# Two feed-forward blocks behind attention: the magnitude step of the second weight block queued behind the exponentials on ScalarE

## The chip, the cores and the metric

The kernel runs on one core of a Trainium2 chip. Five engines work side by side, each through its own instructions in order: TensorE (PE, matrix products), VectorE (DVE), ScalarE (ACT), GpSimd (POOL) and SyncE (SP, which issues the loads here). The metric is the device time of one execution in microseconds (us); the time given is the median of three runs.

## What is computed

Attention over 8 heads and 2 batches (576 positions, 64 dimensions), a sum of a coarse attention over positions averaged by four and of a local one within three positions; then a feed-forward layer of width 2048 with a squared rectifier; then a mixture of four experts of width 1024.

```python
x = attn_ref(q, k, v)                     # 1152 x 512, coarse + local attention
r = np.maximum(x @ w_in, 0.0)
g = s * (r * r) + b
x = g @ w_out
p = domain_probs / domain_probs.sum(-1, keepdims=True)
for e in range(4):
    h = np.maximum(x @ w1[e], 0.0)
    out += p[:, e:e + 1] * (h @ w2[e])
```

The weights of the first layer, `w_in` and `w_out`, come as 64-bit floats, which the kernel takes as pairs of 32-bit words.

## The kernel before

**The stages.** Attention comes first, in 16 units: a unit is two heads of one half of a batch, and four units make a group of columns. The feed-forward layer runs in four blocks of 512 hidden columns, and each block has two layers: layer 1 makes four chunks of hidden values, and layer 2 multiplies them with the second weights. Block 0 is done group by group while attention still runs: as soon as the four units of a group are done, its layer 1 and layer 2 products (L316) are strewn between the next units' steps. Blocks 1 to 3 and the mixture of experts follow.

**A unit's steps** are spread over the passes of one loop (`for i in range(last + 1)`): scores of one unit are written ahead (`b_step`, with the exponentials `exps` at L571 on ScalarE), then the transposes of the probabilities (`c_step`, L657 and L660), the products with the values (`d_step`, L678, L685, L694, L701), and the rounding into the layer's input (`x_step`: L713 on ScalarE, then L715 on POOL). For every other group POOL also makes the averaged keys and values (L474, L475, L539, L541). VectorE takes maxima (L615, L617) and normalises (L630 to L635).

**A hidden chunk** (`moe1_l1`) goes from TensorE through L767 (rectifier, ScalarE), L769 (square and scale, VectorE), L772 (the high part of `h`, ScalarE) and L773 (its low part, VectorE). Each layer 2 product takes three terms of every chunk, in the order high, low, high (`PAIRS`). L793 copies the layer 2 sum away.

**A weight quarter** is converted by `prep`: the magnitude of the high word (`magnitude`, L157, ScalarE), a clamp (L161), a shift (L167) and two joinings with the raw words (L175 and L186, all on VectorE), the high part (L196, ScalarE) and the low part (L199, VectorE), behind which the next raw quarter is loaded into the freed buffer (L122, SP). The steps are taken one at a time from a list (`side_step`) after an attention step or a piece of a block. A block has four quarters, named (block, layer, half). Those of block 1's layer 1, (1, 0, 0) and (1, 0, 1), enter the list at pass i = 12, those of its layer 2 after the loop.

**What sets the order.** The kernel is written in this order, but a scheduler that knows dependences and an estimate of the durations sorts the instructions on each engine; so a step that is written late can be queued early where its inputs are there. `tc.issue_after(x)` holds an instruction back in that sorting until `x` has been placed. On POOL the order is that of the code (`manual_schedule`).

Of the kernel before, what the change touches and what calls it, by code (L numbers as in the profile page):

```python
# [8 lines left out]
F32 = mybir.dt.float32  # L9
# [3 lines left out]
ACTF = mybir.ActivationFunctionType  # L13
# [9 lines left out]
def attn_moe_moe_kernel(  # L23
# [14 lines left out]
    nc = tc.nc  # L38
# [36 lines left out]
    def window(n):  # L75

        return min(max(n * TQ - FAC, 0), S - W)

    def f32(ap):
        return ap.bitcast(F32)  # L80
# [19 lines left out]
    def load_next():  # L100
        if not stream:
            return
        n, which, half = stream.pop(0)
        wi, wo, f0 = blocks[n]
        m = 2 if n < n_moe1 else 1
        dt = I32 if n < n_moe1 else F32
        if n < n_moe1:
            wi, wo = wi.bitcast(I32), wo.bitcast(I32)
        f0 += half * 256
        if which == 0:  # L110
            src = wi[:, f0 * m : (f0 + 256) * m].rearrange("(k p) f -> p k f", p=P)
        else:
            src = wo[f0 : f0 + 256, :].rearrange("(c p) d -> p c d", p=P)
        if n < n_moe1:
            t = rawp.tile([P, 2048], dt, tag="raw", name="raw")
        else:
            if "raw2" not in pools:
                t = rawp.tile([P, 2048], dt, tag="raw", name="raw2")
                pools["raw2"] = [t[:, :1024], t[:, 1024:]]
            t = pools["raw2"].pop(0)  # L120
            pools["raw2"].append(t)
        nc.sync.dma_start(out=t.rearrange("p (a b) -> p a b", a=src.shape[1]), in_=src)  # L122
        raw[n, which, half] = t
# [4 lines left out]
    def w_slot(which):  # L128
        i = places[which].pop(0)
        places[which].append(i)  # L130
        if i < 3 - which:
            pool = wp1 if which else wp0
        else:
            pool = pools["wy" if which else "wx"]
        return [
            pool.tile([P, 1024], F32R, tag=f"w{which}{c}{i}", name=f"w{which}{c}", bufs=1)
            for c in range(2)
        ]

    def prep(n, which, half):  # L140

        if n >= n_moe1:
            return prep2(n, which, half)
        parts = w_slot(which)
        wt[n, which, half] = parts
        st = {}

        def words():
            w = raw[n, which, half].rearrange("p (n two) -> p n two", two=2)
            return w[:, :, 0], w[:, :, 1]  # L150

        def magnitude():
            f = rawp.tile([P, 1024], F32, tag="cv", name="cv")
            st["f"] = f
            nc.scalar.activation(out=f, in_=words()[1].bitcast(F32), func=ACTF.Abs)  # L157

        def clamp():
            f = st["f"]  # L160
            nc.vector.tensor_scalar(  # L161
                out=f, in0=f, scalar1=2.0**-15, scalar2=122879.9921875, op0=ALU.max, op1=ALU.min
            )

        def join():
            c = st["f"].bitcast(I32)
            nc.vector.tensor_scalar(  # L167
                out=c,
                in0=c,
                scalar1=5,  # L170
                scalar2=2,
                op0=ALU.logical_shift_left,
                op1=ALU.logical_shift_right,
            )
            nc.vector.scalar_tensor_tensor(  # L175
                out=c,
                in0=words()[0],
                scalar=29,
                in1=c,
                op0=ALU.logical_shift_right,  # L180
                op1=ALU.bitwise_or,
            )

        def sign():
            c = st["f"].bitcast(I32)
            nc.vector.scalar_tensor_tensor(  # L186
                out=c,
                in0=words()[1],
                scalar=-(2**30),
                in1=c,  # L190
                op0=ALU.bitwise_and,
                op1=ALU.bitwise_or,
            )

        def high():
            nc.scalar.copy(parts[0], st["f"])  # L196

        def low():
            nc.vector.tensor_tensor(  # L199
                out=parts[1], in0=st["f"], in1=f32(parts[0]), op=ALU.subtract  # L200
            )
            load_next()
            ready.add((n, which, half))


        nonlocal tail
        steps = [magnitude] + tail[:1] + [clamp] + tail[1:] + [join, sign]
        tail = [high, low]
        return steps
# [138 lines left out]
    nc.vector.memset(idle, 0.0)  # L348

    last_pe = {}  # L350
    firsts = []

    def take_slot():
# [44 lines left out]
    def unit(u):  # L398
        g, j = divmod(u, NP)
        b, hf = divmod(g, HALVES)  # L400
        return g, j, b, hf

    def tiles(hf):

        return (0, CUT) if hf == 0 else (CUT, NTQ - CUT)
# [6 lines left out]
    def bank():  # L412
        return psa.tile([P, 512], F32, tag="a", name="psa")
# [137 lines left out]
    def b_step(u):  # L551

        g, j, b, hf = unit(u)
        n0, m = tiles(hf)
        gd = m * TQ // FAC
        qz, qd = st.pop(("q", u))
        kT = st["kT", j]
        kd = st["kd", j]
        pl = ap2.tile([P, MX, W], F32, tag="pl", name="pl")[:, :m]
        ml = ap2.tile([P, MX, 1], F32, tag="ml", name="ml")[:, :m]  # L560
        both = gd == GB
        pd = ap2.tile([P, 2, SD], F32, tag="pd", name="pd")
        md = ap2.tile([P, 2, 1], F32, tag="md", name="md")
        if both:
            pd, md = pd[:, :1], md[:, :1]
        else:
            pd, md = pd[:gd], md[:gd]
        sm = sums[u % 2]

        def exps(out, ps, m, total):  # L570
            nc.scalar.activation(  # L571
                out=out, in_=ps, func=ACTF.Exp, bias=m, scale=1.0, accum_out=total
            )

        ps = [bank()] + ([] if both else [bank()])
        last_pe["att"] = nc.tensor.matmul(
            ps[0][:, : m * W],
            identb.rearrange("p a q -> p (a q)"),
            mask[:, hf * 2 : hf * 2 + m].rearrange("p t w -> p (t w)"),
            start=True,  # L580
            stop=False,
        )
        for _ in range(fill[u] // 448):
            nc.tensor.matmul(
                ps[0][:, : m * W], idle[:, :P], idle[:, : m * W], start=False, stop=False
            )
        for t in range(m):
            k0 = window(n0 + t)
            for a in range(2):
                o = slice(a * D, a * D + D)  # L590
                last_pe["att"] = nc.tensor.matmul(  # L591
                    ps[0][a * TQ : a * TQ + TQ, t * W : t * W + W],
                    qz[o, t * TQ : t * TQ + TQ],
                    kT[o, k0 : k0 + W],
                    start=False,
                    stop=t == m - 1,
                )
        local = ps[0][:, : m * W].rearrange("p (t w) -> p t w", w=W)
        pooled = [] if both else [ps[0][:gd, MX * W : MX * W + SD], ps[1][:gd, :SD]]
        if both:  # L600
            pooled = [ps[0][: 2 * gd, MX * W : MX * W + SD]]
            for a in range(2):
                o = slice(a * D, a * D + D)
                last_pe["att"] = nc.tensor.matmul(
                    ps[0][a * gd : a * gd + gd, MX * W : MX * W + SD],
                    qd[o, :],
                    kd[o, :],
                    start=True,
                    stop=True,
                )  # L610
        else:
            for a in range(2):
                o = slice(a * D, a * D + D)
                last_pe["att"] = nc.tensor.matmul(pooled[a], qd[o, :], kd[o, :], start=True, stop=True)
        nc.vector.tensor_reduce(out=ml, in_=local, axis=AX.X, op=ALU.max, negate=True)  # L615
        for a in range(len(pooled)):
            nc.vector.tensor_reduce(  # L617
                out=md[:, a], in_=pooled[a], axis=AX.X, op=ALU.max, negate=True
            )
        for t in range(m):  # L620
            exps(pl[:, t], local[:, t], ml[:, t], sm[:, t])
        for a in range(len(pooled)):
            exps(pd[:, a], pooled[a], md[:, a], sm[: pd.shape[0], MX + a])
        st["p", u] = pl, pd
# [509 lines left out]
```

## Time and profile before

| | us |
|---|---|
| median of three runs (685.72 to 687.32) | 686.23 |
| the profiled execution | 685.9 |
| its span | 684.1 |
| TensorE busy in the span | 673.0 (98%) |
| VectorE busy | 404.7 (59%) |
| ScalarE busy | 345.2 (50%) |
| POOL busy | 103.0 (15%) |

The span is what the records of the engines cover; the profiled execution's own time is 1.8 us longer. Attention with block 0 lasts to about 135 us, block 1 follows. Busy shares are means over the span: in the first 100 us VectorE and ScalarE are busy for 75% and 69%, behind it for about half.

### The profile page before, as it was taken

The numbers are of one execution on the slowest core, as the hardware profiler recorded it, in microseconds if no ns is written. First come the engines' busy times: TensorE is split into PE (matmuls) and PEld (weight loads), VectorE is DVE, ScalarE is ACT, GpSimd is POOL, SyncE is SP. The second block draws the span as 40 slices with busy tenths as digits, with TensorE's granted clock in tenths as the row PEclk, the third lists the DMA queues.
The fourth block names the chain that finished last, engine by engine and source line by source line (L and its number), as shares of the span: only waits on it lengthen the run. The fifth ranks groups of instructions, "written<-read, shape, count | busy, mean of one in ns | idle before, by whom it ended". The sixth has DMA issues, their size and how long they took to land.

```text
span 684.1 us, 11957 instructions
## 1 busy us (share of the span) xinstructions
PE 673.0 (98%) x4788; PEld 614.5 (90%) x4788; DVE 404.7 (59%) x720; ACT 345.2 (50%) x846; POOL 103.0 (15%) x123
## 2 busy tenths in 40 slices
PE   9879999999999999999999999999999999999997
PEld 6668888999999999999899998898998999988996
DVE  1899878598834425695525645646456365455442
ACT  3777788787956656754443433334234234343220
POOL 4431540100002001021201201210112012010000
PEclk9999999999999999999999999999999999999999
DMA  9975845133500101000301201101102012011012
GB/s 189 229 173 112 145 130 157 63 120 127 184 1 1 32 1 62 1 32 0 86 9 61 63 31 32 62 32 61 32 32 65 29 32 92 27 36 32 1 62 77
DMA packets 54167, 46.43 MB, mean 68 GB/s; under 512 B 32224, under 2 KB 42720, under 8 KB 54112
## 3 DMA queue, kind: packets, MB, share of 16 engines
q1 hardware_dynamic: 54112, 45.67, 24.5%
q8 instruction: 37, 0.61, 0.4%
q14 instruction: 18, 0.15, 0.1%
HBM read 43.31 MB, written 2.36 MB: 67 GB/s over the span
## 4 chain that ended last, share of the span: by engine, by line
PE 89%; DVE 7%; ACT 2%; issue 1%; POOL 1%; POOLq 0%; ACTq 0%
PE psm L316 43%; PE psx L863 26%; PE psx L316 13%; PE psa L361 2%; PE psa L591 1%; PE psa L657 1%; DVE cv L175 1%; PE psa L685 1%; PE psa L512 1%; DVE cv L167 1%; PE psa L494 1%; PE psa L678 1%; DVE cv L186 1%; DVE cv L161 0%; DVE pl L632 0%
## 5 line engine op out<-in xcount | busy, mean ns | idle before, releaser
L316 PE MATMUL psm<-w,h 128*128 128x512 f32 x864 | 208.7, 391 | 0.0
L316 PEld LDWEIGHTS psm<-w,h 128*128 128x128 f32 x864 | 158.5, 188 | 30.0
L863 PE MATMUL psx<-x,w 128*128 128x320 f32 (+1 forms) x768 | 117.7, 296 | 0.0
L863 PEld LDWEIGHTS psx<-x,w 128*128 128x128 f32 x768 | 109.2, 189 | 1.7
L259 POOL TENSOR_TENSOR sw<-raw 128x256 f32<-128x256 f32 x32 | 30.1, 960 | 412.1 <-DMA raw<-in_moe_w_dram 270.3
L878 ACT COPY r<-psx 128x320 f32<-128x320 f32 (+1 forms) x96 | 38.1, 396 | 92.9 <-PE psx L863 92.5
L881 ACT ACTIVATE h<-r 128x320 fp32r<-128x320 f32 (+1 forms) x96 | 42.1, 444 | 82.8 <-DVE r L892 82.8
L934 DVE SCALAR_TENSOR_TENSOR acc<-psm,pr,acc 128x512 f32<-128x512 f32 x63 | 47.2, 749 | 57.1 <-PE psm L316 57.1
L863 PE MATMUL psx<-t,w 128*128 128x320 f32 (+1 forms) x448 | 80.2, 302 | 0.3 <-DVE r L892 0.3
L892 DVE TENSOR_TENSOR r<-psx,r 128x320 f32<-128x320 f32 (+1 forms) x96 | 43.2, 456 | 57.9 <-PE psx L863 56.3
L863 PEld LDWEIGHTS psx<-t,w 128*128 128x128 f32 x448 | 67.0, 188 | 4.6 <-DVE r L892 0.6
L316 PE MATMUL psm<-x,w 128*128 128x320 f32 (+2 forms) x420 | 66.6, 310 | 0.0
L316 PEld LDWEIGHTS psm<-x,w 128*128 128x128 f32 x420 | 62.3, 189 | 0.3 <-issue 0.2
L882 DVE SCALAR_TENSOR_TENSOR h<-r,h 128x320 fp32r<-128x320 f32 (+1 forms) x96 | 48.2, 508 | 18.5 <-ACT h L881 16.4
L316 PE MATMUL psm<-h,w 128*128 128x256 f32 (+2 forms) x360 | 56.1, 305 | 0.3 <-DVE h L773 0.3
L316 PE MATMUL psx<-h,w 128*128 128x384 f32 (+1 forms) x312 | 55.8, 327 | 0.0
L316 PEld LDWEIGHTS psx<-h,w 128*128 128x128 f32 x312 | 52.0, 188 | 0.0
L316 PEld LDWEIGHTS psm<-h,w 128*128 128x128 f32 x360 | 50.9, 190 | 1.0 <-DVE h L773 0.5
L316 PE MATMUL psx<-x,w 128*128 128x384 f32 (+2 forms) x252 | 43.1, 320 | 0.0
L316 PEld LDWEIGHTS psx<-x,w 128*128 128x128 f32 x252 | 40.6, 188 | 0.0
L237 DVE TENSOR_TENSOR w<-raw,w 128x1024 fp32r<-128x1024 f32 x16 | 19.5, 1224 | 26.7 <-ACT w L234 26.7
L780 DVE TENSOR_TENSOR h<-r,h 128x384 fp32r<-128x384 f32 (+2 forms) x40 | 21.6, 541 | 20.9 <-ACT h L779 19.6
(105 smaller groups left out, 865.8 us busy)
## 6 DMA issues: line engine op xcount, KB each, us to landing
raw<-in_moe_w_dram SPq DMA_DIRECT2D x32, 512.0 KB
raw<-in_moe_w_in_dram SPq DMA_DIRECT2D x8, 1024.0 KB
raw<-in_moe_w_out_dram SPq DMA_DIRECT2D x8, 1024.0 KB
kn<-in_k_dram SPq DMA_DIRECT2D x8, 288.0 KB
v<-in_v_dram SPq DMA_DIRECT2D x8, 288.0 KB
out_dram<-acc SPq DMA_DIRECT2D x9, 256.0 KB
qn<-in_q_dram SPq DMA_DIRECT2D x8, 160.0 KB
vn<-in_v_dram SPq DMA_DIRECT2D x16, 72.0 KB
```

The source lines that it names most:

```text
L167: nc.vector.tensor_scalar(out=c, in0=c, scalar1=5, scalar2=2, op0=ALU.logical_shift_left, op1=ALU.logical_shift_right,)
L237: nc.vector.tensor_tensor(out=k0[1], in0=source(), in1=f32(k0[0]), op=ALU.subtract)
L259: nc.gpsimd.tensor_tensor(out=operand(out), in0=operand(x), in1=operand(y), op=op)
L316: nc.tensor.matmul(o, stat(ps, kk), mov(pm, kk, i), start=c == 0, stop=c == len(terms) - 1)
L361: nc.tensor.matmul(ps[:, c0:], idle[:, :P], idle[:, :n], start=True, stop=True)
L780: nc.vector.tensor_tensor(out=h[1], in0=r, in1=f32(h[0]), op=ALU.subtract)
L863: nc.tensor.matmul(ps, s_ap(n, half, a, w, kk), xt[x, pi][b][:, kk], start=first and c == 0, stop=c == len(terms) - 1, skip_group_check=True,)
L878: nc.scalar.copy(t, st[name])
L881: nc.scalar.activation(out=h[0][:, halves[hf]], in_=t, func=ACTF.Relu)
L882: nc.vector.scalar_tensor_tensor(out=h[1][:, halves[hf]], in0=t, scalar=0.0, in1=f32(h[0][:, halves[hf]]), op0=ALU.max, op1=ALU.subtract,)
L892: nc.vector.tensor_tensor(out=st[t], in0=st[name], in1=st[t], op=ALU.add)
L934: nc.vector.scalar_tensor_tensor(out=a, in0=ps, scalar=p_e, in1=a, op0=ALU.mult, op1=ALU.add)
```

## The change

The call that writes the magnitude of a quarter is put under `issue_after` where the block is 1, and every exponentials call notes its instruction, so that the four magnitudes of block 1 are placed behind the last exponentials written ahead of them: those of unit 11 and 12 for layer 1, and of unit 15 for layer 2.

```diff
         def magnitude():
             f = rawp.tile([P, 1024], F32, tag="cv", name="cv")
             st["f"] = f
-            nc.scalar.activation(out=f, in_=words()[1].bitcast(F32), func=ACTF.Abs)
+            with tc.issue_after(last_act["att"].ins) if n == 1 else nullcontext():
+                nc.scalar.activation(out=f, in_=words()[1].bitcast(F32), func=ACTF.Abs)
...
+    last_act = {}
...
         def exps(out, ps, m, total):
-            nc.scalar.activation(
+            last_act["att"] = nc.scalar.activation(
                 out=out, in_=ps, func=ACTF.Exp, bias=m, scale=1.0, accum_out=total
             )
```

The line numbers of the new kernel are one more behind L157 and two more behind L350. The scheduler sorts again, so more rows move than the four that are held.

In the rows below `cv` is a quarter's buffer under conversion, `raw` its raw words, `w` with a number its high and low parts; `r` and `h` belong to a hidden chunk, `pl` and `pd` to the probabilities of a unit.

VectorE before, where the first magnitude of block 1 stood at 61 us of the trace (`cv_1590`; `w11_306` is the last quarter of block 0, `h_897` with `r_975` the low part of a fourth chunk):

```order
L769 SCALAR_TENSOR_TENSOR r_975<-r_975,s_sb_90 128x256
L701 TENSOR_TENSOR xg_1003<-psa_981,ud_1001 128x320
L630 TENSOR_SCALAR sum0_106<-sum0_106 128x7
L161 TENSOR_SCALAR cv_1590<-cv_1590 128x1024
L773 SCALAR_TENSOR_TENSOR h_897<-r_975,b_sb_91,h_896 128x256
L631 RECIPROCAL sum0_106<-sum0_106 128x7
L615 TENSOR_REDUCE ml_1052<-psa_1055 128x5
L199 TENSOR_TENSOR w11_306<-cv_788,w10_305 128x1024
L632 TENSOR_TENSOR pl_918<-pl_918,sum0_106 128x360
```

The same place on VectorE in the changed kernel:

```order
L771 SCALAR_TENSOR_TENSOR r_975<-r_975,s_sb_90 128x256
L703 TENSOR_TENSOR xg_1003<-psa_981,ud_1001 128x320
L632 TENSOR_SCALAR sum0_106<-sum0_106 128x7
L633 RECIPROCAL sum0_106<-sum0_106 128x7
L200 TENSOR_TENSOR w11_306<-cv_788,w10_305 128x1024
L775 SCALAR_TENSOR_TENSOR h_897<-r_975,b_sb_91,h_896 128x256
L634 TENSOR_TENSOR pl_918<-pl_918,sum0_106 128x360
```

The clamp of block 1 is gone from here, and the low part of block 0's last quarter stands ahead of the fourth chunk's low part, no longer behind it.

TensorE before, at the same place (`psm_1019` is the layer 2 sum that takes the fourth chunk; `kn` and `idle` rows are an attention unit's transposes and fillers, of which the middle is left out):

```order
L614 MATMUL psa_1056<-kd3_485,qd_960 80x144
L316 MATMUL psm_1113<-h_858,w10_303 128x256
L494 MATMUL psa_1082<-ident_79,kn_910 128x96 x3
...
L494 MATMUL psa_1090<-ident_79,kn_910 128x96
L316 MATMUL psm_1019<-h_896,w10_305 128x256
L316 MATMUL psm_1019<-h_897,w10_305 128x256
...
L316 MATMUL psm_1019<-h_896,w11_306 128x256
L316 MATMUL psm_1019<-h_896,w10_305 128x256
L316 MATMUL psm_1019<-h_897,w10_305 128x256
L316 MATMUL psm_1019<-h_896,w11_306 128x256
```

TensorE there in the changed kernel:

```order
L616 MATMUL psa_1055<-kd3_485,qd_960 80x144
L317 MATMUL psm_1019<-h_896,w10_305 128x256
L317 MATMUL psm_1019<-h_897,w10_305 128x256
L616 MATMUL psa_1056<-kd3_485,qd_960 80x144
L496 MATMUL psa_1082<-ident_79,kn_910 128x96 x3
...
L317 MATMUL psm_1019<-h_896,w11_306 128x256
L317 MATMUL psm_1019<-h_896,w10_305 128x256
L496 MATMUL psa_1090<-ident_79,kn_910 128x96 x2
L317 MATMUL psm_1019<-h_897,w10_305 128x256
L317 MATMUL psm_1019<-h_896,w11_306 128x256
```

All six products of the third and fourth chunk have moved ahead of the second set of the unit's transposes and fillers.

ScalarE before, from the exponentials of unit 11 to the fourth chunk of the third group (`h_1614`; the third chunk is the one with `r_1616`, the fourth the one with `r_1666`):

```order
L571 ACTIVATE pd_1569,sum1_107<-psa_1571,md_1570 128x144
L767 ACTIVATE r_1616<-psm_1601 128x320
L694 ACTIVATE ud_1638<-psa_1622 128x64
L772 ACTIVATE h_1614<-r_1616,b_sb_91 128x320
L660 COPY pT_1642<-psa_1643 72x512
L660 COPY pT_1642<-psa_1649 72x256
L713 CAST x0_76<-xg_1640 128x256
L767 ACTIVATE r_1666<-psm_1653 128x320
L196 CAST w00_1565<-cv_1718 128x1024
L772 ACTIVATE h_1614<-r_1666,b_sb_91 128x320
```

The same stretch of ScalarE in the changed kernel:

```order
L573 ACTIVATE pd_1569,sum1_107<-psa_1571,md_1570 128x144
L158 ACTIVATE cv_1590<-raw_908 128x1024
L769 ACTIVATE r_1616<-psm_1601 128x320
L696 ACTIVATE ud_1638<-psa_1622 128x64
L662 COPY pT_1642<-psa_1643 72x512
L662 COPY pT_1642<-psa_1649 72x256
L774 ACTIVATE h_1614<-r_1616,b_sb_91 128x320
L715 CAST x0_76<-xg_1640 128x256
L769 ACTIVATE r_1666<-psm_1653 128x320
L521 ACTIVATE qz_1725<-psa_1720 128x320
L774 ACTIVATE h_1614<-r_1666,b_sb_91 128x320
L197 CAST w00_1563<-cv_1590 128x1024
```

The magnitude stands ahead of both rectifiers, the two copies of the probabilities ahead of the third chunk's high part, and the conversion's high part has gone behind the fourth chunk.

VectorE before, over the same two chunks:

```order
L769 SCALAR_TENSOR_TENSOR r_1616<-r_1616,s_sb_90 128x320
L632 TENSOR_TENSOR pl_1567<-pl_1567,sum1_107 128x288
L701 TENSOR_TENSOR xg_1640<-psa_1622,ud_1638 128x256
L773 SCALAR_TENSOR_TENSOR h_1615<-r_1616,b_sb_91,h_1614 128x320
L635 TENSOR_TENSOR pd_1569<-pd_1569,sum1_107 128x144
L769 SCALAR_TENSOR_TENSOR r_1666<-r_1666,s_sb_90 128x320
L615 TENSOR_REDUCE ml_1690<-psa_1693 128x5
L617 TENSOR_REDUCE md_1692<-psa_1693 80x1
L773 SCALAR_TENSOR_TENSOR h_1615<-r_1666,b_sb_91,h_1614 128x320
```

VectorE there in the changed kernel:

```order
L162 TENSOR_SCALAR cv_1590<-cv_1590 128x1024
L771 SCALAR_TENSOR_TENSOR r_1616<-r_1616,s_sb_90 128x320
L703 TENSOR_TENSOR xg_1640<-psa_1622,ud_1638 128x256
L168 TENSOR_SCALAR cv_1590<-cv_1590 128x1024
L775 SCALAR_TENSOR_TENSOR h_1615<-r_1616,b_sb_91,h_1614 128x320
L176 SCALAR_TENSOR_TENSOR cv_1590<-raw_908,cv_1590 128x1024
L771 SCALAR_TENSOR_TENSOR r_1666<-r_1666,s_sb_90 128x320
L187 SCALAR_TENSOR_TENSOR cv_1590<-raw_908,cv_1590 128x1024
L775 SCALAR_TENSOR_TENSOR h_1615<-r_1666,b_sb_91,h_1614 128x320
```

The four conversion steps of the quarter stand between the steps of the two chunks; the order on POOL is the same as before. On TensorE, seven small products of the unit (L678 and L685) now stand between the tenth and the eleventh product of that layer 2 group. The other quarters of block 1 move in the same way: the second of layer 1 behind the exponentials of unit 12, the two of layer 2 behind those of unit 15, with their loads on SP behind them.

## Rows read from the trace of the kernel before

**Rows 1.** Page, part 2: granted TensorE clock in 40 slices (9: 90% or more).
```profile
PEclk9999999999999999999999999999999999999999
```
**Rows 2.** Table by stretches: length, then busy (count) by engine, clock, DMA share, GB/s.
```profile
100.00:132.00 32.00, 31.73 (x404) 28.34 (x403) 24.33 (x53) 24.86 (x96) 5.16 (x6) 1.00 0.42 131
132.00:305.00 173.00, 173.00 (x1113) 172.82 (x1112) 108.10 (x169) 119.17 (x225) 7.84 (x9) 1.00 0.17 56
```
**Rows 3.** List of TensorE's waits: us in total, times, longest.
```profile
PE psm L316 <- DVE h L773: 0.3, 1, 0.3
```
**Rows 4.** Timeline, TensorE, from 62 us: start, length, instruction, count.
```profile
62.51 0.48 PE L614 MATMUL psa<-kd,qd 64*80 64x144 f32 x4
...
63.14 0.41 PE L494 MATMUL psa<-ident,kn 96*128 96x96 f32 x3
63.39 0.45 PE L361 MATMUL psa<-idle 128*128 128x224 bf16 x3
63.68 0.25 PE L494 MATMUL psa<-ident,kn 96*128 96x96 f32 x1
...
65.38 1.44 PE L316 MATMUL psm<-h,w 128*128 128x256 f32 x10
```
**Rows 5.** Timeline, ScalarE, from 61 us.
```profile
61.12 1.19 ACT L157 ACTIVATE cv<-raw 128x1024 f32<-128x1024 f32 x1
...
63.50 0.49 ACT L713 CAST x<-xg 128x320 fp32r<-128x320 f32 x1
```
**Rows 6.** Timeline, VectorE, from 62 us; in brackets idle time before and what ended it.
```profile
62.34 0.69 DVE L161 TENSOR_SCALAR cv<-cv 128x1024 f32<-128x1024 f32 x1 [0.21 <-ACT cv L157]
...
63.86 1.21 DVE L199 TENSOR_TENSOR w<-cv,w 128x1024 fp32r<-128x1024 f32 x1
64.99 1.20 DVE L632 TENSOR_TENSOR pl<-pl,sum 128x360 f32<-128x360 f32 x1
```
**Rows 7.** Timeline, POOL, from 62 us.
```profile
64.08 1.72 POOL L715 TENSOR_TENSOR x<-xg,x 128x320 fp32r<-128x320 f32 x1 [17.71 <-ACT x L713]
```
**Rows 8.** Timeline, TensorE, layer 2 of the third group.
```profile
99.36 2.05 PE L316 MATMUL psm<-h,w 128*128 128x320 f32 x12
```
**Rows 9.** Timeline, ScalarE, from 95 us.
```profile
95.45 0.46 ACT L767 ACTIVATE r<-psm 128x320 f32<-128x320 f32 x1
...
97.72 0.41 ACT L713 CAST x<-xg 128x256 fp32r<-128x256 f32 x1
...
99.32 0.56 ACT L772 ACTIVATE h<-r,b_sb 128x320 fp32r<-128x320 f32 x1
```
**Rows 10.** Timeline, VectorE, from 96 us.
```profile
96.77 0.42 DVE L701 TENSOR_TENSOR xg<-psa,ud 128x256 f32<-128x256 f32 x1
97.12 0.55 DVE L773 SCALAR_TENSOR_TENSOR h<-r,b_sb,h 128x320 fp32r<-128x320 f32 x1
...
98.50 0.79 DVE L769 SCALAR_TENSOR_TENSOR r<-r,s_sb 128x320 f32<-128x320 f32 x1 [0.61 <-ACT r L767]
...
99.92 0.88 DVE L773 SCALAR_TENSOR_TENSOR h<-r,b_sb,h 128x320 fp32r<-128x320 f32 x1
```
**Rows 11.** Timeline, POOL, from 98 us.
```profile
98.21 0.73 POOL L715 TENSOR_TENSOR x<-xg,x 128x256 fp32r<-128x256 f32 x1 [3.04 <-ACT x L713]
98.90 1.54 POOL L474 TENSOR_TENSOR v<-v 72x512 f32<-72x512 f32 x1
100.52 0.86 POOL L475 TENSOR_TENSOR vd<-v 72x256 f32<-72x256 f32 x1
```
**Rows 12.** Timeline, VectorE: a joining step of a quarter.
```profile
75.45 1.22 DVE L175 SCALAR_TENSOR_TENSOR cv<-raw,cv 128x1024 int32<-128x1024 int32 x1
```
**Rows 13.** Timeline, TensorE: first products of block 1, and of its layer 2.
```profile
140.80 5.35 PE L316 MATMUL psm<-x,w 128*128 128x320 f32 x31
...
165.59 1.72 PE L316 MATMUL psx<-h,w 128*128 128x384 f32 x9
```
**Rows 14.** Timeline, VectorE: low parts of block 1's layer 2 quarters.
```profile
134.90 2.36 DVE L199 TENSOR_TENSOR w<-cv,w 128x1024 fp32r<-128x1024 f32 x2 [1.07 <-ACT w L196]
```

## Prediction

> **What bounds the kernel now.** I read the granted clock first: TensorE ran at its full level, 2.4 GHz, in every slice [rows 1]. So the time is not the clock's; it is TensorE's work and its gaps. The table by stretches comes next: between 100 and 132 us TensorE is busy for 31.73 of 32 us, and between 132 and 305 us for 173.00 of 173 [rows 2]. The reader is to see two things there. TensorE bounds all that the change touches, so work taken off ScalarE or VectorE gives nothing back by itself: the idle time that could be saved from 100 to 305 us is 0.3 us, and that is the one wait of the list, 0.3 us for `h` written at L773 [rows 3]. And since no gap follows up to 305 us, a delay of TensorE before 132 us has nowhere to be made good and arrives at the end whole. So the question is only whether the moved activations make TensorE wait.
>
> **What the change removes.** L157 for the first quarter of block 1 leaves 61.12 us on ScalarE, where it took 1.19 us [rows 5], and L161 leaves VectorE at 62.34 us (0.69 us) [rows 6]; the second quarter's go likewise. TensorE waited for none of it, so the gain is nothing in itself. But what stands behind it moves up: the order shows that L196 and L713 come about 1 us earlier on ScalarE, that L199 (1.21 us [rows 6]) now stands ahead of L773 of the fourth chunk on VectorE, and that TensorE takes that chunk's products about 1.5 us earlier.
>
> **Place A, 62 to 65 us.** In the new order L196 takes L157's place at 61.2 us and ends near 62.25, so L199 runs from 62.3 to 63.5 and L773 can begin at 63.4. POOL's L715 follows L713, which ends near 63.0 instead of 64.0 [rows 5]. L715 takes 0.86 us alone; here it took 1.72, because it came at 64.08 while L199 ran to 65.07, and L632, which came at 64.99, took 1.20 us while L715 ran to 65.80 [rows 6, 7]. So the two engines shut each other out for a whole instruction and take turns (place B has more such rows). In the new order L715 waits for L199, runs to 64.2, and L773 behind it ends near 64.55. TensorE's way to the low product of the fourth chunk is, from 62.51: 0.2 for the first half of L614, 0.25 for two products (ten in 1.44 us), 0.2 for the other half, 0.54 for three transposes and three fillers (63.14 to 63.68), 0.3 for two products and 0.2 for two transposes, so 64.2 [rows 4]. **It waits 0.4 us.** Without the shutting out L773 would end at 63.8 and the wait would be nothing.
>
> **Place B, 95 to 105 us.** This is the large term. The group of second-layer products that starts at 99.36 us takes 12 products in 2.05 us [rows 8]. Its tenth needs the fourth chunk's `h` high (L772) and its eleventh the low half (L773), and today's margin is slim: the tenth goes out 1.4 us into the row, at 100.8, L772 ended at 99.88 [rows 9], and L773 ended at 100.80 [rows 10], just as it was wanted. The chain before is L767, L769, L772, L773. The new order puts L157 of 1.14 us ahead of the third chunk's L767 on ScalarE, and L161, L167, L175 and L186 between the L769s and L773s on VectorE. I follow it with TensorE, and the exponentials that wait for it, 0.4 us late from place A:
> - the exponentials end at 95.9 (they gave way to L767 at 95.45 [rows 9]); L157 runs to 97.0; L161 (0.69) to 97.75;
> - L769 of the third chunk (0.55) to 98.2, L701 (0.42 [rows 10]) to 98.5, L167 (taken as L161's 0.69) to 99.15, L773 of the third chunk (0.55) to 99.6;
> - on ScalarE L767, L694, two L660 and L772 follow L157, so L713 ends near 99.1, not 98.1 [rows 9], and POOL's three instructions, which begin at 98.21 today [rows 11], come 1 us later;
> - they then meet VectorE at L175 and L186 (1.22 us each [rows 12]) and not at the L615 and L617, which read PSUM. In turns: POOL L715 (0.73) to 100.2; L175 to 101.35; POOL L474 (1.26: today's 1.54 less the 0.28 that L769 held it off) to 102.5; **L769 of the fourth chunk** to 102.95; L772 (0.56 [rows 9]) to 103.55;
> - TensorE wants it at 100.8 + 0.4 = 101.2 and gets it at 103.5: **a wait of 2.3 us**;
> - POOL L475 (0.86 today, of which L773 held it off for 0.14 [rows 10, 11]) to 103.55, L186 to 104.7, L773 of the fourth chunk to 105.2. TensorE has one product and seven small ones between (0.7 us), so it stands again at 104.25: **0.9 us more**.
>
> The turns are what I take from the trace: L769 at 98.50 took 0.79 us while POOL's L715 ran to 98.94, and L773 at 99.92 took 0.88 us while L474 ran to 100.44, where the same form at 97.12, with POOL idle, took 0.55; L474, issued at 98.90, took 1.54 us because L769 held it off to 99.3 [rows 10, 11]. The engine that waited came next each time. If VectorE's next instruction went first whenever it is ready, POOL would wait for the end of the row of them, and the sum would be the first rival's.
> The Trainium skill, "SBUF — State Buffer", section "SBUF: two separate sides", says that VectorE with two SBUF inputs and GpSimd share a port pair as an exclusive lock, which the one that starts first holds for its whole instruction. The trace agrees on the lock with 0.88 against 0.55 us. It does not say who goes next when VectorE's queue is full; were that always VectorE, the sum would be the first rival's 686.5, and the turns give 689.2.
>
> **Later.** The second quarter's L157 comes behind the next unit's exponentials at about 107 us, with no second-layer chunk to feed there. The two of block 1's second layer come at about 129 us, one of them ahead of L772 of the last group's fourth chunk; TensorE is by then 3.6 us late and the other engines have that much room: 0.1 us at most. For the same reason the 0.3 us of [rows 3], a wait for L773 in that group, goes. The quarters themselves stay early: block 1's first products run in the last two thirds of the row at 140.80 [rows 13], and their low half is ready at about 108, L199 being four short instructions behind L773; the second layer's are wanted at 165.59 [rows 13], and today's L199 ran at 134.90 (2.36 us for two [rows 14]), tomorrow's some 6 us later. The loads behind them on SP's queue move with L199 and have over 20 us in hand.
>
> **Sum.** 0.4 + 2.3 + 0.9 - 0.3 = 3.3 us on the profiled execution's 685.9 us, which stands 0.3 us under the median of the three runs (686.23): 689.2 us.
>
> **Rivals.**
> - *The engines do not shut each other out in the new order, or POOL's instructions fall between.* Then L175 ends at 100.75, L769 at 101.2, L772 at 101.75: a wait of 0.5 us, then L773 at 102.85 against 102.5: 0.35; place A costs nothing, and 0.3 us is saved: +0.6, 686.5 us, no difference that shows. The point from which it decides is POOL's L715: if it is served before L167, or behind L769 of the fourth chunk. For it: some rows overlap freely, those that read PSUM. Against it: each row in which the forms concerned met shows the delay.
> - *It gets faster.* All that could be won from 100 to 305 us is the 0.3 us of [rows 3], so 685.6 us; for over 0.2% (1.4 us, about what a measurement of this kernel can tell from no change) no idle time is there.
> - *The two late L157 bite too.* If at 129 us TensorE has no room, L157 (1.14 us) and L161 stand ahead of the last group's L772 and L773: +1.2 us, 690.4 us. It speaks against it that all producers have the 3.6 us.
>
> **How the numbers follow.** The forecast, with both waits at place B, has 0.68; the first rival and forms between it and a half-sized wait 0.20; the faster one 0.05; the slower one 0.07. The range goes from the first rival's low side, 686.3, to the last one's with the spread of the runs, 690.9. Slower by over 0.2% is above 687.6: 0.73; within: 0.23; faster: 0.04.
>
> **What would show it.** In the profile after, the list of TensorE's waits should name L772 and L773 (a line or two further down in the new numbering) with 2 to 3.5 us in all, between 100 and 106 us; POOL's L474 near 100 us should last over 2 us, and L175 or L186 beside it 1.8 us. TensorE's busy share from 132 us on should be as before, shifted. It is wrong if that list shows no such wait, if block 1's first products wait for their weights near 142 us, or if the clock falls.

## The result

The changed kernel takes 691.53 us (median of four runs, 689.05 to 693.13) against 686.22 us before (four runs, 685.72 to 687.32): a ratio of 1.0074, 95% interval 1.0054 to 1.0094. It is slower, as forecast, but by 5.3 us where 3 were forecast, and the median lies 0.6 us above the stated range.

The profiled execution took 689.05 us (span 687.3), 0.15 us from the forecast of 689.2. It was the quickest of the four, and the only one in which the mean granted clock was as high as in the profile of before:

| granted clock, mean over a run | runs of the changed kernel (four, and six more of the same kernel), us |
|---|---|
| 0.999 | 689.05 |
| 0.997 | 690.17 |
| 0.995 | 690.48, 691.23, 691.96 |
| 0.993 | 691.22, 691.35, 692.55 |
| 0.990 | 692.57, 693.13 |

Of the 44 runs of before made in the experiments, 43 lie between 0.996 and 1.000 and one is at 0.995, and the median of each batch is 686.1 to 686.2 us; three of them reach 688.3 to 688.8 us, at 0.996 and 0.997. A mean of 0.997 says little by itself: 28 of the 44 are at 0.997 or below, and the profile of the run that holds only layer 2's quarters, at 0.997, has its one fall near 48 us, far ahead of the places of the change. What sets the changed kernel apart is 0.995 and less, in eight of its ten runs. The order of the table is not strict: 691.96 us at 0.995 stands above two runs at 0.993.

The page after, parts 1 and 2, is like the one before but for the span; what has changed is the list of TensorE's waits (us in total, times, longest), which before had, for `h` of layer 2, one entry of 0.3 us for L773 [rows 3]. L774 and L775 are the L772 and L773 of before.

```profile
PE psm L317 <- DVE h L775: 1.5, 1, 1.5
...
PE psm L317 <- ACT h L774: 1.1, 1, 1.1
```

The timeline of TensorE shows where (start, length, instruction, count; in brackets the idle time and what ended it). The twelve products of [rows 8] are now nine, one and two:

```profile
97.58 0.85 PE L593 MATMUL psa<-kT,qz 64*64 64x72 f32 x20
...
99.06 1.57 PE L317 MATMUL psm<-h,w 128*128 128x320 f32 x9
101.76 0.42 PE L317 MATMUL psm<-h,w 128*128 128x320 f32 x1 [1.13 <-ACT h L774]
102.10 0.46 PE L680 MATMUL psa<-pT,vd 72*64 72x64 f32 x8
102.39 0.40 PE L687 MATMUL psa<-pT,vn 72*64 72x64 f32 x6
104.30 0.56 PE L317 MATMUL psm<-h,w 128*128 128x320 f32 x2 [1.52 <-DVE h L775]
...
107.83 0.32 PE L578 MATMUL psa<-mask,identb 64*128 64x360 bf16 x1
```

VectorE beside it, where `cv` rows are the steps of the quarter that was moved here:

```profile
98.48 0.55 DVE L775 SCALAR_TENSOR_TENSOR h<-r,b_sb,h 128x320 fp32r<-128x320 f32 x1
98.95 1.22 DVE L176 SCALAR_TENSOR_TENSOR cv<-raw,cv 128x1024 int32<-128x1024 int32 x1
100.08 1.03 DVE L771 SCALAR_TENSOR_TENSOR r<-r,s_sb 128x320 f32<-128x320 f32 x1
101.03 2.28 DVE L187 SCALAR_TENSOR_TENSOR cv<-raw,cv 128x1024 int32<-128x1024 int32 x1
103.24 1.01 DVE L775 SCALAR_TENSOR_TENSOR h<-r,b_sb,h 128x320 fp32r<-128x320 f32 x1
```

And POOL:

```profile
98.60 2.16 POOL L717 TENSOR_TENSOR x<-xg,x 128x256 fp32r<-128x256 f32 x1 [3.58 <-ACT x L715]
100.72 1.51 POOL L476 TENSOR_TENSOR v<-v 72x512 f32<-72x512 f32 x1
102.31 1.59 POOL L477 TENSOR_TENSOR vd<-v 72x256 f32<-72x256 f32 x1
```

The three POOL instructions took 0.73, 1.54 and 0.86 us before [rows 11]. L717 and L477 now wait for a step of the conversion and L476 for L771, and each holds the next VectorE instruction off: L187 takes 2.28 us where a joining step takes 1.22 [rows 12], and L771 and L775 take 1.0 where 0.55 is their own length [rows 10].

At 62 to 65 us, where a wait of 0.4 us was forecast (place A), TensorE shows none. TensorE, then VectorE:

```profile
61.90 0.47 PE L616 MATMUL psa<-kd,qd 64*80 64x144 f32 x2
62.30 0.50 PE L317 MATMUL psm<-h,w 128*128 128x256 f32 x2
62.73 0.47 PE L616 MATMUL psa<-kd,qd 64*80 64x144 f32 x2
63.13 0.47 PE L496 MATMUL psa<-ident,kn 96*128 96x96 f32 x3
...
64.09 0.48 PE L317 MATMUL psm<-h,w 128*128 128x256 f32 x2
```

```profile
62.90 1.08 DVE L775 SCALAR_TENSOR_TENSOR h<-r,b_sb,h 128x256 fp32r<-128x256 f32 x1
```

The fourth chunk's low part was ready at 63.98 us, and its product, the first of the row at 64.09, came to it no earlier. What costs time here is TensorE's own new order: before, the four L614 products ran in one row of 0.48 us [rows 4]; parted by two products of layer 2, each two of them keep the next row off for 0.40 us (61.90 to 62.30, 62.73 to 63.13).

A word on names: the group whose layer 2 waits at 100 us is the second of the four (its columns are 320), which the sections above call the third; the group at 129 us, there the last, is the third.

### The profile page after: what moved, and what is told of

It is laid out like the page before. It is cut to its first block, busy times and chain, and to the rows that moved or that the text cites. A ratio compares the mean times of both kernels' runs of the same rounds, so it can differ in the third digit from the quotient of the medians.

```text
span 687.3 us, 11954 instructions
## 1 busy us (share of the span) xinstructions
PE 673.0 (98%) x4788; PEld 614.0 (89%) x4788; DVE 405.5 (59%) x720; ACT 344.5 (50%) x846; POOL 104.1 (15%) x123
## 4 chain that ended last, share of the span: by engine, by line
PE 88%; DVE 7%; ACT 3%; issue 1%; DMA 1%; SPq 0%; ACTq 0%
PE psm L317 42%; PE psx L865 26%; PE psx L317 13%; PE psa L363 1%; PE psa L659 1%; PE psa L593 1%; DMA kn<-in_k_dram 1%; PE psa L687 1%; ACT pl L573 1%; DVE cv L187 1%; DVE pl L634 1%; PE psa L514 1%; DVE cv L168 1%; PE psa L680 0%; PE psa L496 0%
```

## The experiments

**The same kernel again**, and a profile of another of its executions.

> The changed kernel as it is. Its profiled execution took 689.05 us at a granted clock of 0.999, its other three runs 690.48 to 693.13 us at 0.990 to 0.995. Theory A: the two waits of TensorE at 100 to 104 us (1.3 and 1.7 us) cost 3.2 us in every run, and behind them the clock is lowered in some runs, which costs 1.5 to 4 us more: runs of 689 us at 0.999 and runs of 690 to 693 us at 0.990 to 0.996, none in between that breaks the order. Theory B: the clock has nothing to do with the change and falls in runs of the kernel before as often: then before shows runs of 688 us and more at 0.990 to 0.996 as well.

Measured: 691.29 us (six runs, 690.17 to 692.55), ratio 1.0075 (1.0060 to 1.0091), clocks of 0.993 to 0.997. Its profile fell on a run of 692.55 us, and differs from the first in two ways, the waits and the clock. TensorE, from the same nine products on:

```profile
99.94 1.56 PE L317 MATMUL psm<-h,w 128*128 128x320 f32 x9
103.70 0.41 PE L317 MATMUL psm<-h,w 128*128 128x320 f32 x1 [2.20 <-ACT h L774]
104.04 0.64 PE L680 MATMUL psa<-pT,vd 72*64 72x64 f32 x8
104.44 0.63 PE L687 MATMUL psa<-pT,vn 72*64 72x64 f32 x6
105.23 0.90 PE L317 MATMUL psm<-h,w 128*128 128x320 f32 x2 [0.16 <-DVE h L775]
...
108.85 2.54 PE L317 MATMUL psm<-h,w 128*128 128x320 f32 x9
111.32 0.32 PE L578 MATMUL psa<-mask,identb 64*128 64x360 bf16 x1
```

Table by stretches (length, then busy and count of PE, PEld, DVE, ACT and POOL, then the granted clock): this execution, three stretches.

```profile
95.00:104.00 9.00, 6.80 (x78) 5.74 (x73) 8.31 (x14) 5.68 (x19) 4.94 (x4) 1.00 0.17 39
104.00:112.00 8.00, 7.84 (x58) 6.60 (x59) 5.78 (x13) 6.18 (x22) 0.00 (x0) 0.57 0.48 156
112.00:120.00 8.00, 8.00 (x104) 6.93 (x100) 6.82 (x13) 5.83 (x23) 0.72 (x1) 1.00 0.23 44
```

The same middle stretch of the first profile of the changed kernel:

```profile
104.00:112.00 8.00, 7.70 (x85) 6.60 (x87) 7.00 (x18) 7.38 (x32) 0.74 (x1) 1.00 0.46 154
```

Here one wait of 2.2 us stands in place of 1.1 and 1.5, and behind it TensorE runs at its lower level, 1.2 GHz, from about 104.2 to 111.0 us: 58 products instead of 85, and nine products take 2.54 us, not 1.56. From the tenth product to L578 it takes 111.32 - 103.70 = 7.62 us, 7.46 without the 0.16 us wait; in the first profile the same way took 107.83 - 101.76 = 6.07, 4.55 without the 1.52. So the lowered clock cost **2.9 us** here. Of the 3.5 us between the two executions another 0.9 were lost earlier (the nine products start at 99.94 us, not 99.06); this profile also has the fall near 48 us, the first has not. Theory A holds for this execution; the idle time before the fall is so far only what stands next to it.

VectorE and POOL in this execution show why the waits fell out differently:

```profile
99.36 0.54 DVE L775 SCALAR_TENSOR_TENSOR h<-r,b_sb,h 128x320 fp32r<-128x320 f32 x1
99.82 1.76 DVE L176 SCALAR_TENSOR_TENSOR cv<-raw,cv 128x1024 int32<-128x1024 int32 x1
101.51 1.54 DVE L771 SCALAR_TENSOR_TENSOR r<-r,s_sb 128x320 f32<-128x320 f32 x1
102.97 1.74 DVE L187 SCALAR_TENSOR_TENSOR cv<-raw,cv 128x1024 int32<-128x1024 int32 x1
104.64 0.54 DVE L775 SCALAR_TENSOR_TENSOR h<-r,b_sb,h 128x320 fp32r<-128x320 f32 x1
```

```profile
99.48 1.02 POOL L717 TENSOR_TENSOR x<-xg,x 128x256 fp32r<-128x256 f32 x1 [3.59 <-ACT x L715]
100.47 2.24 POOL L476 TENSOR_TENSOR v<-v 72x512 f32<-72x512 f32 x1
```

L717 was issued 0.12 us behind L775 in both executions. In this one it went ahead of L176, which took 1.76 us; in the first one L176 kept its 1.22 and L717 took 2.16. Everything behind it follows in turn, as forecast, but from the other engine on. Who goes first there is not settled by the order; two executions of one program differ in it.

**One half of the change at a time.**

```diff
-            with tc.issue_after(last_act["att"].ins) if n == 1 else nullcontext():
+            with tc.issue_after(last_act["att"].ins) if (n, which) == (1, 1) else nullcontext():
```

> Only the magnitudes of block 1's layer 2 quarters are held behind the exponentials; those of layer 1 stand as before. Theory A: no wait at 100 to 104 us, the 0.3 us wait near 126 us may grow to 1 us: 686 to 687 us, clock 0.999 in all runs. Rival (the two late activations near 129 us matter): 688 us and more, with waits for L774 and L775 between 126 and 132 us, and a lowered clock if any gap does it.

Measured: 685.87 us (twelve runs), ratio 0.9992 (0.9979 to 1.0005). No wait at L774 or L775 is in its list, and the 0.3 us of [rows 3] is gone. Holding the layer 2 quarters costs nothing. The clock of its profile is down only near 48 us, at 1.2 GHz from about 48.5 to 52 us, behind a wait of 2.0 us for `qd` that the profile of before has too, there at a clock of 1.00 throughout. This execution's stretch from 0 to 54 us:

```profile
0.00:54.00 54.00, 47.33 (x514) 36.55 (x515) 36.20 (x76) 31.91 (x111) 20.85 (x34) 0.97 0.93 194
```

```diff
+            with tc.issue_after(last_act["att"].ins) if (n, which) == (1, 0) else nullcontext():
```

> Only the magnitudes of block 1's layer 1 quarters are held. Theory A: both waits at 100 to 104 us are there and the time is that of the changed kernel, 689 us at 0.999 and up to 693 us with the clock lowered. Rival (the later pair carries it): 686 to 687 us.

Measured: 693.61 us (six runs), 1.0098 (1.0073 to 1.0122), clocks of 0.993 to 0.995. Its list has 2.2 us for L774 and 0.5 for L775, and TensorE's mean clock is 0.82 from 104 to 112 us. The whole loss is in the layer 1 half. It came out above the full change; some of that is the start of its profiled execution, which was some 3 us late at 95 us already, from a cause that no run here shows, and the rest is left open.

**Work in place of the idle time.** Products of zeros are put where TensorE waits.

```diff
         for c, (kk, ps, pm) in enumerate(terms):
+            for _ in range(zeros[1] if zeros and c == zeros[0] else zeros[3] if zeros and c == zeros[2] else 0):
+                nc.tensor.matmul(outs[0], idle[:, :P], idle[:, : outs[0].shape[1]], start=False, stop=False)
...
+            (9, 9, 10, 12) if (n, g, dc) == (0, 1, 0) else None,
```

> The changed kernel with 9 and 12 products of zeros (320 columns, 0.13 us each) ahead of the tenth and the eleventh product of the layer 2 group that waits at 100 us, so that TensorE works through most of the two waits. Theory A: the waits are filled and not shortened, so the time is 689 us and up to 0.8 us more, and the clock stays at 0.999 in every run: the runs of 690.5 to 693 us are gone. Theory B (the lowered clock is not from the idle TensorE): runs at 0.990 to 0.996 and up to 693 us stay as frequent as in the changed kernel.

Measured: 692.23 us (six runs), 1.0094 (1.0074 to 1.0115), clocks 0.998, 0.998, 0.998, 0.998, 1.000 and 1.000. The clock did what theory A says: none of the six is at 0.995 or below, where eight of ten runs of the changed kernel are. The time did not: the zeros took their own room (1.40 and 1.80 us), 0.5 us of the second wait was left, and the scheduler drew the small products behind them, after which a wait of 1.15 us for `qd` stood at 116 us. Its profiled execution was also 1.2 us behind that of before at 98 us, ahead of the zeros. From there to the next unit's mask product (L580 here, L578 in the changed kernel) it took 10.9 us, against 13.1 in the execution with the lowered clock and 10.5 in the first one. So the clock follows the idle time of TensorE; the fill kept it up at this place, but the kernel as a whole gained nothing.

**POOL's part.** The changed kernel without the two value additions of unit 11 (that unit takes the averaged values of another one); the order on ScalarE, VectorE and TensorE is unchanged.

```diff
-        if hf == 0:
+        if hf == 0 and u != SKIP:
             vd = ap1.tile([ND, 2, 2, D], F32, tag=f"vd{j}", name=f"vd{j}")
```

> The changed kernel without POOL's two additions of the averaged values of unit 11 (72x512 and 72x256), which stand beside the conversion steps at 100 us; unit 11 then uses the values of another unit, and the order on the other engines is the same. Theory A (the waits come from VectorE and POOL shutting each other out): POOL's L717 alone is left, so L771 of the fourth chunk ends 1.2 us earlier where POOL goes first, and L187 and L775 are not held off: the waits come to 0.9 to 1.9 us in all, instead of 2.4 to 2.9; with them the clock should be lowered less often, and the time is 687 to 689 us. Rival (the waits are the conversion steps' own length): unchanged, 691 to 693 us.

Measured: 688.13 us (seven runs), 1.0039 (1.0025 to 1.0053); five runs at 0.998 or above, two at 0.993 (690.00 and 690.23). The slowest, 690.42 us at 0.998, is the profiled one; it came to this place some 3 us late already. TensorE waits 1.19 us for L776 (the same `h` high) and not at all for the low part:

```profile
104.88 0.41 PE L317 MATMUL psm<-h,w 128*128 128x320 f32 x1 [1.19 <-ACT h L776]
105.22 0.46 PE L682 MATMUL psa<-pT,vd 72*64 72x64 f32 x8
105.50 0.40 PE L689 MATMUL psa<-pT,vn 72*64 72x64 f32 x6
```

```profile
102.01 1.76 DVE L176 SCALAR_TENSOR_TENSOR cv<-raw,cv 128x1024 int32<-128x1024 int32 x1
103.69 0.54 DVE L773 SCALAR_TENSOR_TENSOR r<-r,s_sb 128x320 f32<-128x320 f32 x1
104.15 1.21 DVE L187 SCALAR_TENSOR_TENSOR cv<-raw,cv 128x1024 int32<-128x1024 int32 x1
```

L176 still meets POOL's remaining instruction; L773 and L187 are back at their own lengths. Two POOL instructions of about 1.3 us (the prediction's estimate) and 0.7 us, on an engine that is busy for 15% of the span, carry 3.2 us of the change's cost. The first rival of the prediction, that the engines don't shut each other out, falls.

**The same wait without the change.** One more POOL addition, of zeros, in the kernel before, ahead of unit 11's additions; TensorE's order is that of before. Three lengths.

```diff
+            if u == 11:
+                nc.gpsimd.tensor_tensor(out=junk, in0=junk, in1=junk, op=ALU.add)
```

> The kernel before with one more POOL addition, of zeros to zeros (72x1024, about 2.5 us), ahead of unit 11's first value addition. TensorE's order is that of before. Theory A: it holds L773 of the fourth chunk off until about 102 us, so TensorE waits once, for 1.1 us; the clock stays up, and the time is 687 us. Rival (a POOL addition doesn't hold VectorE): 686.2 us and no wait.

Measured with 1024 columns: 688.43 us (seven runs), 1.0033 (1.0021 to 1.0046). The addition took 2.14 us and L777 (before's L773) 1.47; TensorE waited 0.4 us there, and 1.6 us for `qd` afterwards. Two of seven runs are at 0.993 and 0.994. Less than half the expected wait, with a second one that was not expected.

> As the run with 1024 columns, with 1536 (about 3.8 us). Theory A: L773 is held off until 103.3 us, TensorE waits once for 2.4 us, as in the changed kernel, and nothing else of the change is there; behind the wait the clock falls to its lower level for 3.4 or 6.8 us in most runs, which costs 1.7 to 3.4 us: 688.5 us with the clock up, 690 to 692 us with it lowered. Theory B (the clock does not depend on this wait): 688.5 us, and a lowered clock no more often than before.

Measured with 1536: 688.71 us (eleven runs, 686.61 to 691.18), 1.0037 (1.0024 to 1.0050). The addition took 2.99 us, not 3.8, so the wait was 1.21 us, not 2.4. Three of eleven runs are at 0.995, the profiled one among them: its clock is at the lower level from about 104.2 to 107.6 us. Eight are at 0.998, and so are the two slowest, 690.54 and 691.18 us: the clock is not all that differs between runs. Half an answer.

> The kernel before with the extra POOL addition at 2176 columns; with 1536 it took 2.99 us and TensorE waited 1.2 us for L773 of the fourth chunk. By 0.85 us for 512 columns it takes 4.0 us here and the wait is 2.3 us, as in the changed kernel where POOL went first (2.2 us). Theory A (a wait of this length brings the clock down behind it): the clock is at its lower level for 3.4 or 6.8 us behind the wait in more runs than at 1.2 us, where 3 of 11 runs showed a mean clock of 0.995: at least half the runs at 0.995 or below, and a median of 689.5 to 691 us. Theory B: clock as in before (0.997 to 1.000), 688.5 us.

Measured with 2176: **691.27 us** (five runs, 690.59 to 693.53), 1.0080 (1.0066 to 1.0094), all five clocks at 0.995 or below (0.990 to 0.995). POOL, VectorE and TensorE of its profile:

```profile
99.00 4.06 POOL L551 TENSOR_TENSOR junk<-junk 72x2176 f32<-72x2176 f32 x1
```

```profile
100.02 3.39 DVE L777 SCALAR_TENSOR_TENSOR h<-r,b_sb,h 128x320 fp32r<-128x320 f32 x1 [0.19 <-ACT h L776]
```

```profile
103.46 0.59 PE L316 MATMUL psm<-h,w 128*128 128x320 f32 x2 [2.28 <-DVE h L777]
...
106.61 3.55 PE L316 MATMUL psm<-h,w 128*128 128x320 f32 x12
```

```profile
104.00:112.00 8.00, 8.00 (x71) 6.83 (x71) 3.12 (x8) 5.16 (x20) 2.00 (x3) 0.58 0.48 154
```

An instruction of 0.55 us lasted 3.39 beside one POOL addition; TensorE waited once at this place, for 2.28 us, and then worked at a mean clock of 0.58 for 8 us (1.2 GHz from about 103.9 to 110.7 us), where twelve products take 3.55 us instead of 2.05 [rows 8]. Nothing of the change is in this kernel, and it is as slow as the changed one: 5.0 us for a wait of 2.3. In the profile, TensorE takes 5.25 us more than before from the unit's mask product at 97.74 us to the next at 110.09: 2.28 of waiting and some 3 behind it. That is the missing term, by itself.

**The quarters one by one, and one pass later.**

```diff
+            with tc.issue_after(last_act["att"].ins) if (n, which, half) == (1, 0, 0) else nullcontext():
```

> Only the first quarter of block 1's layer 1 is held behind the exponentials; the other three stand as before. Theory A: its four steps on VectorE are the ones at 97 to 104 us, so waits for L774 and L775 of 1.5 to 3 us and 689 to 692 us. Rival (it takes both quarters): under 688 us.

Measured: 692.06 us (four runs), 1.0078 (1.0057 to 1.0098); waits of 0.3 us for L774 and 2.1 for L775 at 101 to 104 us, and a lowered clock behind them. One quarter is enough for the whole loss.

> Only the second quarter of block 1's layer 1 is held. Theory A: no wait at 100 us beyond before's, 686 to 687 us. Rival: over 688 us.

(The edit is the same with half 1.) Measured: 689.51 us (four runs), 1.0053 (1.0033 to 1.0072). No wait at 100 us, but four later ones:

```profile
116.74 0.30 PE L659 MATMUL psa<-ident,pl 128*72 128x128 f32 x1 [0.31 <-DVE qd L528]
...
119.65 0.31 PE L578 MATMUL psa<-mask,identb 64*128 64x360 bf16 x1 [0.85 <-ACT pd L573]
...
125.40 0.71 PE L659 MATMUL psa<-ident,pl 128*72 128x128 f32 x5 [0.61 <-DVE pl L634]
...
129.30 0.50 PE L317 MATMUL psm<-h,w 128*128 128x256 f32 x2 [0.83 <-ACT h L774]
```

The second quarter's steps, too, make TensorE late where it is on time. In the full change none of these waits is there; TensorE comes 3 us later to that place, which would give the other engines the room; that is argued, not shown.

```diff
+        if i == NU - NP + 1:
             side += prep(1, 0, 0) + prep(1, 0, 1)
```

> The change with the two layer 1 quarters of block 1 put into the list one pass of the loop later, so that their magnitudes stand behind the exponentials of the units 12 and 13, where no layer 2 product of block 0 waits for a chunk. Theory A (it is the place that costs, not the holding): no wait of TensorE for L774 or L775 of over 0.5 us, 686 us like before, clock as before. Rival (any later place runs into TensorE's needs): 688 us and more, with the wait at another chunk or at the weights of block 1.

Measured: 689.96 us (six runs), 1.0052 (1.0040 to 1.0064). The wait at 100 us is gone as expected, and others have come: 0.53 us at 112.57, 0.43 at 116.67 and 0.42 at 133.86 us, for `qd`, `pT` and `pd`. They add up to 1.4 us; its profiled execution, of 690.81 us, was 1.9 us behind that of before at 97 us already, ahead of them. Theory A was wrong on this: it is not that one place. A quarter's five steps on VectorE, some 5 us, meet a TensorE without a gap at both places tried; where they stand before, TensorE waits for none of it.

## Why the prediction was right or wrong

- **What bounds it: right.** TensorE's delay before 132 us went through to the end: from 138 to 308 us it is busy for 170.00 of 170 us.
- **Place A: a right size by luck, the wait was not there.** The chain on VectorE and POOL went as forecast: L775 took 1.08 us beside POOL's L717 and ended 2.1 us after the first L616 began, forecast 2.0. But TensorE's own way to the low product took 2.2 us, not 1.7: the prediction gave each half of L614 0.2 us, half of the row of four, and parted each takes 0.4. So TensorE did not wait, and lost 0.5 us by its order: it was 0.61 us ahead of before's profile at 60.61 us (L578, before 61.22) and 0.08 at 70.69 (before 70.77).
- **Place B: right in mechanism, somewhat too large in the waits.** Forecast 2.3 and 0.9 us, 3.2 in all. In one execution 2.20 and 0.16 with the small products slowed between, in another 1.13 and 1.52: 2.4 and 2.65. Not in the sum was what the new order costs with the clock up: from L578 at 97.33 us to the next at 107.83 TensorE takes 10.50 us, before 7.10, so 0.75 more than the waits (the twelve products alone 1.57 + 0.42 + 0.56 in place of 2.05 us). The turns were a right guess, with one thing left out: who starts them is open where both come within 0.12 us.
- **Later: right in size, not in its reasons.** No wait stands between 105 and 305 us, the 0.3 us went, and no weight came late. For the late pair and the 0.3 us the reason named was that TensorE is late. But the run that holds only layer 2's quarters has TensorE within 0.3 us of before's profile from 61 to 119 us, and neither wait is there; and the kernel with the addition of 2176 columns, 5.6 us late, still waits 0.27 us for that `h`. For the second quarter the reason was that no chunk is to be fed there; alone it costs 3.3 us, with four waits of 2.6 us in its profile, for `qd`, `pd`, `pl` and `h`.
- **The sum: this is the step that failed.** "0.4 + 2.3 + 0.9 - 0.3" prices each idle microsecond at one. It took the clock from [rows 1] as given, named a falling clock only among what would make the prediction wrong, and gave it neither a rival nor a price. The runs put a term in its place: 2.9 us behind the 2.2 us wait, and 5.0 us in all for a wait of 2.3 us with nothing else changed. With it the sum is 3.3 to 6.2 us, and the median's 5.3 lies in it. [rows 1] holds for the execution that it was read from, at 0.999; 28 of 44 runs of before are at 0.997 or below, so their clock did fall somewhere. The first profiled execution of the changed kernel had no fall either and came out at 689.05 us; that this is 0.15 us from the forecast is in part luck, with the 0.61 us by which it was ahead at 60.61 us.
- **The range** reached to 690.9 for mishaps of a microsecond; a rival of its own, the clock falling behind place B, would have ended near 692.
- **The rivals.** The first fell with the run without POOL's additions; the slower one (the late pair of quarters) with the run that holds only these.

The Trainium skill, "SBUF — State Buffer", section "SBUF: two separate sides", has VectorE and GpSimd take their common port pair for whole instructions; 3.39 us for an instruction of 0.55 us agrees.

## What to carry to other kernels

A TensorE that never idles has a clock to lose. A wait of 2 us put into such a stretch costs its own length and, in the profiles here that show the fall right behind it, some 3 us more at the lower clock, and an estimate needs a term for it even where the profile of before shows the full clock throughout: that is one execution. A time that comes out right is no proof of its parts, as place A shows: put every term beside its own row. Work that is off the critical path should be judged by what stands in the same queues where it lands, POOL's small instructions among them, and not by whether its result is in time.

## What the runs showed of the hardware

- Behind a wait of TensorE of 2.1 to 2.3 us, in a stretch almost without other gaps, the clock was at 1.2 GHz for several microseconds (mean clock 0.57, 0.57 and 0.58 from 104 to 112 us in three profiles). Of the kernels with a wait of 1.2 us only some runs show a lowered mean (two of seven, three of eleven). With two waits, of 1.1 and 1.5 us and 1 us of work between, the profiled run kept 1.00.
- Two executions of one program differ in whether VectorE or POOL goes first at the same spot, and with it in how TensorE's wait is cut.
- All kernels here wait for `qd` for 2.0 us near 48 us. In some executions, of kernels with and without the change, the clock falls there as well: from 0 to 54 us it is 0.97 in the profile of the run that holds only layer 2's quarters (685.96 us, mean 0.997) and 1.00 in that of before (0.999).
- Four products of 64 rows and 80 columns (L614) ran in 0.48 us side by side, and two of them alone in 0.47 us.
